# Another start, load order and instruction order for a squared-relu attention with a mixture of adapters

## The chip, the core and the metric

The kernel runs on one core of a Trainium2 chip. The core has five engines with instruction streams of their own: TensorE (PE, matmuls; its weight loads are listed as PEld), VectorE (DVE), ScalarE (ACT), GpSimd (POOL) and SyncE (SP). POOL, ACT and SP also issue DMA transfers. The metric is the device time of one execution in microseconds; lower is better. The kernel before takes 186.77 us, the median of 13 runs from 185.96 to 189.39.

## The reference

```python
# q, k, v: (8, 12, 448, 64) float32
scores = (1 / sqrt(64)) * q @ k.T                 # per batch and head: 448 x 448
attn   = maximum(scores, 0) ** 2 / 448
x      = (attn @ v), heads side by side            # (3584, 768)

logits = x @ w_gate                                # (3584, 8)
top two experts of each row, w = softmax over the two
out    = x + sum over the two: w[e] * (x @ A[e]) @ B[e]     # A: (8, 768, 16), B: (8, 16, 768)
```

## The kernel before, in words

**Tiling.** A head has 448 rows, split as 7 pieces (J) of 64. Twelve heads are taken four at a time, so there are 8 batches x 3 quads, each a "quad" (b, q) of four heads. A quad's q, k and v each come by one pair of DMA transfers from POOL, cast from fp32 to bf16 on the way (L271). A quad has seven steps, one for each 64 keys; the 168 steps are called chunks below.

**One quad.** PE transposes q and k, 56 matmuls of 64x64 against an identity (L386), and DVE copies the result from PSUM to the tile qT (L400). For each chunk PE computes the scores of four heads, four matmuls of 64x448 (L445), into a pair of PSUM banks. A relu with a scale brings them to SBUF as bf16, tile a (on ACT L465, on DVE L467). DVE squares two or three chunks at a time (L483). PE multiplies the squares with v, four matmuls a chunk (L500), adding up over the seven chunks, and two copies bring the sum to xt (L529, DVE or ACT).

**The adapters.** Two blocks of 36 small matmuls (L338) put A and w_gate, which come as a_raw and g_raw (L323, L325), in their places, by a selection matrix sel that POOL makes (L316, L317); a copy (L345) follows each block. For every 128 rows of x there is a gate product (six matmuls, L546), a few small DVE and ACT steps for the top two (L567 to L590), a transpose (L607) with a copy (zT, L616), and two output halves: three identity matmuls that bring x back (L634), one fp32 matmul with B (L639, which the profile shows as two), a copy to the tile osb (L656), and after both halves two stores from SP's queue (L666). There are 28 such row tiles, so 56 output halves.

**The first quad.** The first three pieces of k (CUT = 3) come uncast by one transfer each on SP's and ACT's queues into raw (L283), and DVE casts them to k_first (L298). The other four come by POOL with the cast into k_rest (L294). ACT loads its table with a sigmoid on a small tile (L287); POOL makes the identity.

**What sets the order.** The program is written as a list of operations with engines, assumed durations, dependencies, buffers taken and given back, and a rank (the chunk for which it is due, with offsets from the table C). A planner, `schedule`, plays this list forward on assumed costs and emits each engine's instructions in the resulting order; each engine then runs in that order. So a different rank, cost or pool size changes the order everywhere. Tile pools bound how far ahead anything runs: q and k 4 buffers, v 6, output tiles 6. The eight PSUM banks are handed out by the planner (scores take pairs). At most four load pairs are in flight (`lane=4`).

Loads are issued on POOL in the order of this loop; a tile of v follows the q and k of the next quad:

```python
    for i in range(len(tiles_of) + 1):
        if i < len(tiles_of):
            loads(i, 0)
            loads(i, 1)
        if i:
            loads(i - 1, 2)
        if i == 2:
            # sel, a_raw and g_raw, B
```

Of the kernel before, what the change touches and what calls it, by code (L numbers as in the profile page):

```python
# [13 lines left out]

J = 7
CUT = 3
PH = 64
QUADS = 3
NB = 8
S = J * PH  # L20
# [10 lines left out]
def parts(*cuts):  # L31
# [3 lines left out]

C = dict(
    tp_=2.3287, qk_=-3.679, sq_=3.7975, pv_=3.3372, xt_=-1.2131, gate_=-0.65203, id_=-0.78412,
    out_=-0.80943, zt_=6.6019, a12=(4, 7), late=6, merge_x=0, id2=2.6063, ocap=3, sqs=(2, 2, 3),
    slack=0.12309, switch=3.3127, third=4.3408, dve_relu=0.55845, relu_until=400, qk=-2.3217, sq=10,
    pv=1.0506, xt=8.4423, tp=-9.2867, tpe=4.3867, gate_mm=-4.8593, gate=-1.4524, zt=0.2432, zte=2.902,  # L40
    id=15.183, out=3.032, pace=6.5353,
)
POOLS = dict(qT=5, a1=C["a12"][0], a2=C["a12"][1], zp=2, zT=3, osb=6, w=3, q=4, k=4, v=6)

MODE_SWITCH = 0.13
HOP = 0.05
RAW = {"PE": 0.0, "ACT": 0.2, "DVE": 0.115, "POOL": 0.0, "SP": 0.0}
LAT = {"PE": 0.18, "ACT": 0.19, "DVE": 0.084, "POOL": 0.0, "SP": 0.0}
# [28 lines left out]
class Dma:  # L77


    def __init__(self, rate=0.4):  # L80
        self.rate, self.free = rate, 0.0

    def land(self, t, mb):
        self.free = max(self.free, t + 0.5) + mb / self.rate
        return self.free + 1.4


def schedule(ops, c=C):

    free = {e: 0.0 for o in ops for e in o.engs}
    avail = {e: [] for e in free}
    level = dict(POOLS, lane=4)
    freed = {b: 0.0 for b in range(c.get("nb", 8))}
    used = {"s": 0, "t": 0, "p": 0, "m": 0, "y": 0, "o": 0}
    cap = {"s": 3, "t": 1, "p": 2, "m": 2, "y": 1, "o": c.get("ocap", 1)}
    events, returns = [0.0], []
    dma = Dma()
    mode = None  # L100
    relus = []
# [13 lines left out]
    def choose(o):  # L115
        k, n = o.want
        if used[k] >= cap[k]:
            return None
        slots = sorted((x for x in range(0, c.get("nb", 8), 2) if x in freed and x + 1 in freed),
                       key=lambda x: max(freed[x], freed[x + 1]))  # L120
        if k == "s":
            if used["s"] >= 2 and any(
                x.want and x.kind != "qk" and x.ready <= t + 1e-9 and x.rank <= o.rank + c["third"]
                for x in avail["PE"]
            ):
                return None
            return [slots[0], slots[0] + 1] if slots else None
        halves = sorted((x for x in freed if x ^ 1 not in freed), key=lambda x: freed[x])
        if n == 1 and halves:
            return halves[:1]  # L130
        busy = c.get("nb", 8) // 2 - len(slots) - used["s"]
        if not slots or busy >= c.get("nb", 8) // 2 - 2:
            return None
        if n == 1 and busy == 1 and any(
            x.want and x.ready <= t + 1e-9 and x.kind in ("pv", "tp") and x.rank <= o.rank
            for x in avail["PE"]
        ):
            return None
        return [slots[0], slots[0] + 1][:n]
# [19 lines left out]
    while left:  # L159
# [9 lines left out]
        for e in free:  # L169
# [8 lines left out]
                    st = max(t, free[e] + MODE_SWITCH)  # L178
                mode = o.mode
            o.start, o.eng = st, e  # L180
            free[e] = st + o.dur[e]
            if o.kind == "load":
                o.end = dma.land(free[e], o.mb) + (o.lat or 0.0)
            else:
                o.end = free[e] + (LAT[e] if o.lat is None else o.lat)
            for x in o.engs:
# [41 lines left out]
def build(k=None, c=C):  # L228
# [49 lines left out]
    def first():  # L278

        def dma(eng, g):
            eng.dma_start(out=k.raw[g * PH : g * PH + PH], in_=k.qkv[1][0, g, :, 0:2, : CUT * PH])  # L283

        def warm():
            nc.vector.memset(k.warm, 0.0)
            nc.scalar.activation(k.warm, k.warm, ACTF.Sigmoid)  # L287

        def ident():
            make_identity(nc, k.identf)  # L290

        def rest():
            for g in range(2):
                nc.gpsimd.dma_start(out=k.k_rest[g * PH : g * PH + PH],  # L294
                                    in_=k.qkv[1][0, g, :, 0:2, CUT * PH :])

        def cast():
            nc.vector.tensor_copy(k.k_first, k.raw)  # L298

        ds = [op(("SP",), 0.8, lambda: dma(nc.sync, 0), kind="load", rank=-50.0),  # L300
              op(("ACT",), 0.8, lambda: dma(nc.scalar, 1), kind="load", rank=-50.0)]
        for d in ds:
            d.mb = 2 * CUT * PH * 64 * 4e-6
        op(ACT, 1.4, warm, rank=-49.0)
        q0 = load(0, 0, 0, [])
        oi = op(("POOL",), 0.6, ident)
        ob = op(DVE, 0.2, lambda: nc.vector.tensor_copy(k.identb, k.identf), deps=[oi], rank=-60.0)
        k0 = op(DVE, dve(2 * CUT * PH, 1.92), cast, deps=ds + [ob], rank=-50.0)
        k1 = op(("POOL",), 1.17, rest, kind="load", take=("lane",), give=("lane",))
        k1.mb = 4 * (S - CUT * PH) * 64 * 4e-6  # L310
        return q0, k0, k1


# [62 lines left out]
    def tp(b, q):  # L376
# [34 lines left out]
        if (b, q) == (0, 0):  # L411
            kw = dict(mode="64", kind="tp")
            m1 = op(PE, 0.1, lambda: mm(m1, 1, 0, CUT), deps=[loaded[b, 1, q][0]], ni=8 * CUT, banks=("s", 2),
                    take=("qT",), rank=-52.0, **kw)
            m = op(PE, 0.225, lambda: mm(m, 0), deps=[loaded[b, 0, q]], after=m1, ni=56, banks=("t", 2),
                   rank=-51.0, **kw)
            m2 = op(PE, 0.13, lambda: mm(m2, 1, CUT), deps=[loaded[b, 1, q][1]], after=m, ni=8 * (J - CUT),
                    banks=("s", 2), give=("q",), rank=-8.0, **kw)
            e1 = op(DVE, dve(2 * CUT * PH, 1.92), lambda: piece(nc.vector.tensor_copy, m1, 1, 0, CUT), deps=[m1],
                    free=[(m1, None)], rank=-42.0)  # L420
            es = [op(x, {"ACT": act(S), "DVE": dve(S, 1.92)},
                     lambda cp=cp, g=g: piece(cp, m, 0, 0, J, g), deps=[m, e1], free=[(m, g)], rank=-41.0)
                  for g, (x, cp) in enumerate(((DVE, nc and nc.vector.tensor_copy), (ACT, nc and nc.scalar.copy)))]
            e2 = op(DVE, dve(2 * (J - CUT) * PH, 1.92), lambda: piece(nc.vector.tensor_copy, m2, 1, CUT, J),
                    deps=[m2, es[0]], free=[(m2, None)], rank=-5.0)
            return [[e1, *es] + [e2] * (j >= CUT) for j in range(J)]
        m = op(PE, 0.225, lambda: mm(m, 0), deps=[loaded[b, 0, q]], mode="64", kind="tp", ni=56,
               banks=("t", 2), take=("qT",), rank=rank)
        m1 = op(PE, 0.225, lambda: mm(m, 1), deps=[loaded[b, 1, q], m], after=m, mode="64", kind="tp", ni=56,
                give=("k", "q"), rank=rank - 0.5)  # L430
        e = op(DVE, dve(4 * S, 1.92), ev, deps=[m1], free=[(m, None)], rank=rank + c["tpe"])
        return [[e]] * J

# [189 lines left out]
    def outputs(tl):  # L623
# [3 lines left out]
        v = due[tl]  # L627
        W = 64 * DO
        evs, obs, prev = [], {}, None
        for h in range(2):  # L630

            def f_b(h=h):
                for x in range(3):
                    nc.tensor.matmul(  # L634
                        out=bank(obs[h])[:, x * 128 : x * 128 + 128],
                        lhsT=k.xt[:, 3 * h + x, c0 : c0 + 128], rhs=k.identb,
                        start=(x == 0), stop=False, skip_group_check=True,
                    )
                nc.tensor.matmul(  # L639
                    out=bank(obs[h])[:, :W], lhsT=T["zT", g0][:, zi], rhs=k.B[:, h * W : h * W + W],  # L640
                    start=False, stop=True, skip_group_check=True,
                )

            last = False
            if h:
                zuse[g0] -= 1
                last = zuse[g0] == 0
            prev = op(PE, 0.81, f_b, mode="128", kind="b", deps=[o_zT, b_load] + xdeps[tl], after=prev,
                      banks=("o", 1), take=() if h else ("osb",), give=("zT",) if last else (),
                      rank=v + at("id", v) + (c["id2"] if h else 0), ni=10)  # L650
            obs[h] = prev

            def ev(cp, h=h):
                if ("osb", tl) not in T:
                    new("osb", ("osb", tl), [128, 128 * DO], F32)
                cp(T["osb", tl][:, h * W : h * W + W], bank(obs[h])[:, :W])  # L656

            evs.append(evac(W, ev, deps=[prev], free=[(prev, 0)], rank=v + at("out", v)))

        def st():  # L660
            r = 0
# [18 lines left out]
        if (b, w, q) not in loaded:  # L680
            loaded[b, w, q] = load(b, w, q, [])

    for i in range(len(tiles_of) + 1):
        if i < len(tiles_of):
            loads(i, 0)
            loads(i, 1)
        if i:
            loads(i - 1, 2)
        if i == 2:
            sel_op = op(("POOL",), 1.5, sel_fn)  # L690
            a_load = op(("POOL",), 1.5, aw_fn, kind="load")
            a_load.mb = 0.4
# [4 lines left out]

    groups, t = [], 0
    while t < NT:
        m = min(3, NT - t)  # L700
        if NT - t == 4:
            m = 2
        if t == NT - 2:
# [41 lines left out]
            finish(n - c["late"] - 1)  # L745
    for n in range(NS - c["late"] - 1, NS):
        finish(n)
    return ops


@with_exitstack
def kernel(
# [31 lines left out]
    h.a_raw = const.tile([128, E, DO, R], BF16)  # L784
    h.g_raw = const.tile([128, DO, E], BF16)
    h.raw = const.tile([128, 2, CUT * PH], F32)
    h.k_first = const.tile([128, 2, CUT * PH], BF16)
    h.k_rest = const.tile([128, 2, (J - CUT) * PH], BF16)
    h.warm = const.tile([1, 8], F32)
# [39 lines left out]
```

## Time and profile before

| | |
|---|---|
| median of 13 runs | 186.77 us |
| the profiled execution's own time | 186.99 us |
| its span, first to last instruction | 185.2 us |
| PE busy | 169.0 us (91%) |
| DVE busy | 159.2 us (86%) |
| ACT busy | 161.0 us (87%) |
| first scores on PE, first relu on ACT | 6.10 us, 6.91 us |
| last scores on PE | 160.16 us |
| last relu on ACT | 160.81 us |
| last output copy | 180.24 us |

The profile cuts the span into 40 slices of 4.63 us and gives the busy share of each engine in tenths. PE, DVE and ACT are all close to full between about 40 and 160 us; before that none of them is, and behind it PE alone is. A group row gives line, engine, operation, tiles, shape and count, then busy time and the mean duration of one, then the engine's idle time just before it and what ended that. A timeline row gives start and duration in us first. A busy PE is not a PE at its peak, since the ends of matmuls are modelled.

### The profile page before, as it was taken

The numbers are of one execution on the slowest core, as the hardware profiler recorded it, in microseconds if no ns is written. First come the engines' busy times: TensorE is split into PE (matmuls) and PEld (weight loads), VectorE is DVE, ScalarE is ACT, GpSimd is POOL, SyncE is SP. The second block draws the span as 40 slices with busy tenths as digits, with TensorE's granted clock in tenths as the row PEclk, the third lists the DMA queues.
The fourth block names the chain that finished last, engine by engine and source line by source line (L and its number), as shares of the span: only waits on it lengthen the run. The fifth ranks groups of instructions, "written<-read, shape, count | busy, mean of one in ns | idle before, by whom it ended". The sixth has DMA issues, their size and how long they took to land.

```text
span 185.2 us, 7480 instructions
## 1 busy us (share of the span) xinstructions
PE 169.0 (91%) x3236; PEld 99.4 (54%) x3236; DVE 159.2 (86%) x249; ACT 161.0 (87%) x234; POOL 90.8 (49%) x155
## 2 busy tenths in 40 slices
PE   0869998789999999999999999999999999999990
PEld 0526765445555646564656465655665566556640
DVE  1569999899999999999999999999999999853600
ACT  3677799899999999999999999999999999954350
POOL 7999789898786856465735744671100000000000
PEclk9999999999999999999999999999999999999996
DMA  5999999999999999799999999899430333344775
GB/s 92 122 168 145 177 161 176 178 182 177 143 232 228 223 185 243 118 175 170 174 186 133 192 185 200 118 193 228 89 86 2 88 88 90 85 106 110 210 196 147
DMA packets 26801, 28.71 MB, mean 155 GB/s; under 512 B 4432, under 2 KB 23120, under 8 KB 26768
## 3 DMA queue, kind: packets, MB, share of 16 engines
q0 software_dynamic: 22000, 17.03, 65.3%
q1 hardware_dynamic: 4624, 11.11, 20.3%
q8 instruction: 25, 0.41, 0.9%
q10 hardware_dynamic: 144, 0.10, 0.2%
q14 instruction: 8, 0.07, 0.1%
HBM read 33.84 MB, written 11.01 MB: 242 GB/s over the span
## 4 chain that ended last, share of the span: by engine, by line
PE 57%; DVE 16%; ACT 13%; issue 4%; POOL 4%; DMA 3%; ACTq 0%; POOLq 0%
PE ps L639 17%; PE ps L445 13%; ACT a L465 12%; PE ps L500 12%; DVE a L483 8%; PE ps L634 6%; PE ps L546 4%; DMA q<-in_q_dram 3%; PE ps L386 3%; DVE qT L400 3%; DVE xt L529 3%; PE ps L338 2%; POOL q L271 1%; PE ps L607 1%; DVE zp L590 1%
## 5 line engine op out<-in xcount | busy, mean ns | idle before, releaser
L465 ACT ACTIVATE a<-ps 128x896 bf16<-128x896 f32 x162 | 139.1, 955 | 5.2 <-PE ps L445 4.9
L483 DVE TENSOR_TENSOR a<-a 128x1792 bf16<-128x1792 bf16 (+1 forms) x72 | 88.3, 1247 | 0.4 <-ACT a L465 0.4
L445 PE MATMUL ps<-qT 64*64 64x448 bf16 x672 | 61.5, 378 | 4.0 <-ACT a L465 2.0
L639 PE MATMUL ps<-B,zT 128*128 128x384 f32 x112 | 48.4, 514 | 0.0
L500 PE MATMUL ps<-a,v 64*64 64x448 bf16 x672 | 44.0, 358 | 0.6 <-DVE qT L400 0.5
L271 POOL DMA_DIRECT2D v<-in_v_dram x48 | 29.1, 621 | 27.2 <-PE ps L500 12.7
L445 PEld LDWEIGHTS <-qT 64*64 64x64 bf16 x672 | 23.5, 107 | 34.4 <-issue 25.6
L271 POOL DMA_DIRECT2D q<-in_q_dram x48 | 29.2, 626 | 8.9 <-PE ps L386 2.4
L271 POOL DMA_DIRECT2D k<-in_k_dram x46 | 28.2, 637 | 3.0 <-PE ps L445 1.9
L500 PEld LDWEIGHTS <-v 64*64 64x64 bf16 x672 | 22.3, 109 | 12.1 <-issue 5.1
L656 ACT COPY osb<-ps 128x384 f32<-128x384 f32 x45 | 22.3, 495 | 7.0 <-PE ps L639 5.9
L529 DVE CAST xt<-ps 128x448 bf16<-128x448 f32 x42 | 24.9, 618 | 3.6 <-PE ps L500 3.2
L400 DVE COPY qT<-ps 128x1792 bf16<-128x1792 bf16 x23 | 24.9, 1083 | 2.1 <-PE ps L386 1.4
L634 PE MATMUL ps<-identb,xt 128*128 128x128 bf16 x168 | 18.8, 221 | 0.1
L634 PEld LDWEIGHTS <-xt 128*128 128x128 bf16 x168 | 11.3, 97 | 13.2 <-issue 11.5
L639 PEld LDWEIGHTS ps<-B,zT 128*128 128x128 f32 x112 | 16.9, 191 | 0.0
L546 PE MATMUL ps<-awg,xt 128*128 128x136 bf16 x168 | 13.4, 224 | 0.0
L386 PEld LDWEIGHTS <-q 64*64 64x64 bf16 x672 | 10.6, 114 | 4.3 <-DMA q<-in_q_dram 1.5
L546 PEld LDWEIGHTS <-xt 128*128 128x128 bf16 x168 | 10.1, 98 | 4.8 <-issue 4.4
L386 PE MATMUL ps<-identb,k 64*64 64x64 bf16 x644 | 11.0, 199 | 1.5 <-DMA k<-in_k_dram 1.5
L386 PE MATMUL ps<-identb,q 64*64 64x64 bf16 x672 | 11.0, 199 | 0.4
L386 PEld LDWEIGHTS <-k 64*64 64x64 bf16 x644 | 9.4, 110 | 3.0 <-DMA k<-in_k_dram 2.5
(41 smaller groups left out, 72.2 us busy)
## 6 DMA issues: line engine op xcount, KB each, us to landing
out_dram<-osb SPq DMA_DIRECT2D x56, 192.0 KB, 3.4
q<-in_q_dram POOLq DMA_DIRECT2D x48, 112.0 KB, 4.7
v<-in_v_dram POOLq DMA_DIRECT2D x48, 112.0 KB, 4.6
k<-in_k_dram POOLq DMA_DIRECT2D x46, 112.0 KB, 5.0
B<-in_moe_B_dram POOLq DMA_DIRECT2D x1, 384.0 KB, 5.6
a_raw<-in_moe_A_dram POOLq DMA_DIRECT2D x1, 192.0 KB, 5.6
k_rest<-in_k_dram POOLq DMA_DIRECT2D x2, 64.0 KB, 2.9
raw<-in_k_dram ACTq DMA_DIRECT2D x1, 96.0 KB, 2.6
```

Source lines behind the costliest of these rows:

```text
L271: nc.gpsimd.dma_start(out=t[g * PH : g * PH + PH], in_=k.qkv[w][b, g, :, 2 * q : 2 * q + 2, :])
L386: nc.tensor.transpose(k.ps_b[sl * PH : sl * PH + PH, o.banks[g], (w * J + j) * PH : (w * J + j) * PH + PH], source(w, j)[r, sl], k.identb[ ...
L400: nc.vector.tensor_copy(t.rearrange("p g w x -> p g (w x)"), k.ps_b[:, m.banks[0] : m.banks[0] + 2, : 2 * S])
L445: nc.tensor.matmul(out=bank(o, sl)[g * PH : g * PH + PH, at : at + w], lhsT=t[r, g, 1, j * PH : j * PH + PH], rhs=t[r, g, 0, x0:x1], start ...
L465: nc.scalar.activation(out, flat(qk_ops[n], w), ACTF.Relu, scale=k.relu_scale)
L483: nc.vector.tensor_mul(a2, T["a1", g0], T["a1", g0])
L500: nc.tensor.matmul(out=bank(head, g)[sl * PH : sl * PH + PH, :w], lhsT=vn[r, sl, j * PH : j * PH + PH], rhs=T["a2", g0][r, i, sl * w : sl ...
L529: evac(w, lambda cp, g=g: cp(k.xt[:, g * QUADS + q, b * S + x0 : b * S + x1], bank(src, g)[:, :w]), deps=[pv_ops[n]], free=[(src, g)], ran ...
L546: nc.tensor.matmul(out=bank(zops[0])[:, t * ZW : t * ZW + ZW], lhsT=k.xt[:, do, 128 * tiles[t] : 128 * tiles[t] + 128], rhs=k.awg[:, do, : ...
L634: nc.tensor.matmul(out=bank(obs[h])[:, x * 128 : x * 128 + 128], lhsT=k.xt[:, 3 * h + x, c0 : c0 + 128], rhs=k.identb, start=(x == 0), sto ...
L639: nc.tensor.matmul(out=bank(obs[h])[:, :W], lhsT=T["zT", g0][:, zi], rhs=k.B[:, h * W : h * W + W], start=False, stop=True, skip_group_che ...
L656: cp(T["osb", tl][:, h * W : h * W + W], bank(obs[h])[:, :W])
```

## The change

At the start, PE multiplies a tile of zeros eight times (`SPIN`) before the first transposes, and eight shorter times between the transposes of the first q and the first scores. The last four pieces of the first k come uncast by two transfers on ACT's queue, behind ACT's table load, and DVE casts them. POOL's loads run in the order q_0, q_1, k_1, q_2, k_2, v_0, and so on: v comes one quad later, sel and a_raw two turns of the loop later. A quad's q transposes now wait for its k as well (`tboth`). Output tiles have 4 buffers instead of 6; q and k 5 instead of 4, v 7 instead of 6. The planner gets other costs for the start and for loads, four other weights, offsets to the ranks of 84 operations, and fixed engines for 12.

```diff
+SPIN = 8
-    out_=-0.80943, zt_=6.6019, a12=(4, 7), late=6, merge_x=0, id2=2.6063, ocap=3, sqs=(2, 2, 3),
-    slack=0.12309, switch=3.3127, third=4.3408, dve_relu=0.55845, relu_until=400, qk=-2.3217, sq=10,
+    out_=-0.80943, zt_=6.6019, a12=(4, 7), late=6, merge_x=0, id2=2.6063, ocap=3, tboth=1, sqs=(2, 2, 3),
+    slack=0.097658, switch=4.846, third=4.5956, dve_relu=0.45964, relu_until=400, qk=-2.3217, sq=10,
-POOLS = dict(qT=5, a1=C["a12"][0], a2=C["a12"][1], zp=2, zT=3, osb=6, w=3, q=4, k=4, v=6)
+POOLS = dict(qT=5, a1=C["a12"][0], a2=C["a12"][1], zp=2, zT=3, osb=4, w=3, q=5, k=5, v=7)
+RANKS = {
+    1: -6, 148: -7, 163: -106, 166: -110, 171: 27, 175: -64, 180: -17, 187: -31, 197: -44, ...
+}
+ENGINES = {
+    170: "DVE", 214: "DVE", 315: "DVE", 330: "DVE", 337: "ACT", 446: "DVE", 547: "DVE", ...
+}
+BEGIN = {"PE": 1.1, "ACT": 0.74, "DVE": 0.8, "POOL": 1.24, "SP": 0.74}
+COLD = 7.0
...
-            free[e] = st + o.dur[e]
+            free[e] = st + o.dur[e] * (2 if e == "PE" and st < COLD else 1)
...
+        def zeros():
+            nc.vector.memset(k.zeros, 0.0)
+        def spin():
+            for _ in range(SPIN):
+                nc.tensor.matmul(k.ps[:, 7, :], lhsT=k.zeros[:, :128], rhs=k.zeros, start=True, stop=True)
         def rest():
             for g in range(2):
-                nc.gpsimd.dma_start(out=k.k_rest[g * PH : g * PH + PH],
-                                    in_=k.qkv[1][0, g, :, 0:2, CUT * PH :])
+                dma(nc.scalar, k.raw_rest, g, CUT, J)
...
+        k1 = op(DVE, dve(2 * (J - CUT) * PH, 1.92), lambda: nc.vector.tensor_copy(k.k_rest, k.raw_rest),
+                deps=[kr], rank=-30.0)
...
+            def spin():
+                for _ in range(2):
+                    for g in range(2):
+                        for sl in range(2):
+                            nc.tensor.matmul(bank(sp, g)[sl * PH : sl * PH + PH, :], lhsT=k.zeros[g * PH : g * PH + PH, :PH],
+                                             rhs=k.zeros[g * PH : g * PH + PH], start=True, stop=True)
...
-    for i in range(len(tiles_of) + 1):
+    for i in range(len(tiles_of) + 2):
         if i < len(tiles_of):
             loads(i, 0)
             loads(i, 1)
-        if i:
-            loads(i - 1, 2)
-        if i == 2:
+        if i > 1:
+            loads(i - 2, 2)
+        if i == 4:
             sel_op = op(("POOL",), 1.5, sel_fn)
...
+    for i, d in RANKS.items():
+        ops[i].rank += d / 4
+    for i, e in ENGINES.items():
+        ops[i].engs = (e,)
```

In the order that comes out, PE begins with eight zero matmuls, the transposes of k_first and q_0, eight short zero matmuls, the scores of chunks 0 to 2, then the transposes of q_1, k_rest and k_1, the scores of chunks 3 to 6, the transposes of q_2 and k_2, and the scores of six chunks of the second quad. Before, it took the second quad's transposes and the first quad's scores in turns: q_1 after chunk 3, k_1 after chunk 5.

## The prediction

> **What bounds the kernel now.** I read, in this order: the page's table of busy time and its 40 slices; the timeline of ACT up to 45 us and the waits there; the groups of PE instructions cut into short windows; busy time by stage; the chain of waits.
>
> ```profile
> PE 169.0 (91%) x3236; PEld 99.4 (54%) x3236; DVE 159.2 (86%) x249; ACT 161.0 (87%) x234; POOL 90.8 (49%) x155
> ...
> PE   0869998789999999999999999999999999999990
> ...
> ACT  3677799899999999999999999999999999954350
> ...
> PEclk9999999999999999999999999999999999999996
> DMA  5999999999999999799999999899430333344775
> ```
>
> Three stages: to about 42 us no engine is full; from there to 160 PE, DVE and ACT are all full; after 160 only PE is. The first stage on ACT (start, duration, operation, and in brackets the idle time before it with its releaser):
>
> ```profile
> 6.91 4.16 ACT L465 ACTIVATE a<-ps 128x896 bf16<-128x896 f32 x5 [0.68 <-PE ps L445]
> 11.83 0.92 ACT L465 ACTIVATE a<-ps 128x896 bf16<-128x896 f32 x1 [0.77 <-PE ps L445]
> 13.24 4.33 ACT L465 ACTIVATE a<-ps 128x896 bf16<-128x896 f32 x5 [0.49 <-PE ps L445]
> ```
> ```profile
> 18.50 2.54 ACT L465 ACTIVATE a<-ps 128x896 bf16<-128x896 f32 x3 [0.93 <-PE ps L445]
> 22.01 1.73 ACT L465 ACTIVATE a<-ps 128x896 bf16<-128x896 f32 x2 [0.97 <-PE ps L445]
> 24.06 4.16 ACT L465 ACTIVATE a<-ps 128x896 bf16<-128x896 f32 x5 [0.32 <-PE ps L445]
> ...
> 33.21 0.92 ACT L465 ACTIVATE a<-ps 128x896 bf16<-128x896 f32 x1 [0.43 <-PE ps L445]
> 34.30 4.97 ACT L465 ACTIVATE a<-ps 128x896 bf16<-128x896 f32 x6 [0.17 <-PE ps L445]
> ```
>
> Each relu without a bracket follows the last at 0.81 to 0.83 us (five in 4.16 with a last one of 0.95). Each bracket is ACT waiting for PE's scores (L445). Between 13.24 and 42 these waits sum to 0.93 + 0.97 + 0.32 + 0.43 + 0.17 = 2.82 us. Why is PE late? Two reasons. It is slow (window 6 to 7 us, then 100 to 110 us, then the change-over):
>
> ```profile
> L445 PE MATMUL ps<-qT 64*64 64x448 bf16 x8 | 1.4, 557 | 0.4 <-DVE qT L408 0.4
> ```
> ```profile
> L445 PE MATMUL ps<-qT 64*64 64x448 bf16 x44 | 3.6, 355 | 0.0
> ```
> ```profile
> 16.70 1.38 PE L500 MATMUL ps<-a,v 64*64 64x448 bf16 x12
> ...
> 18.20 0.73 PE L500 MATMUL ps<-a,v 64*64 64x448 bf16 x8
> ```
>
> The same matmul takes 557 ns early and 355 later; from 18.2 us on it is fast. And PE waits for data:
>
> ```profile
> 10.84 0.58 PE L386 MATMUL ps<-identb,k 64*64 64x64 bf16 x26 [0.56 <-DMA k<-in_k_dram]
> ...
> 13.66 0.13 PEld L386 LDWEIGHTS <-q 64*64 64x64 bf16 x2 [0.86 <-DMA q<-in_q_dram]
> ```
>
> The DMA row is full from the second slice on, so early loads queue for bandwidth, not only for POOL's issue. The last stages (length; busy time and instruction count of PE, PEld, DVE, ACT, POOL; clock; DMA):
>
> ```profile
> 120.00:140.00 20.00, 19.99 (x413) 12.12 (x409) 19.79 (x33) 19.68 (x28) 4.76 (x8) 1.00 0.68 140
> 140.00:160.00 20.00, 20.00 (x361) 11.60 (x354) 19.61 (x31) 19.82 (x32) 0.00 (x0) 1.00 0.25 62
> 160.00:170.00 10.00, 10.00 (x99) 5.99 (x92) 5.80 (x16) 5.72 (x13) 0.00 (x0) 1.00 0.46 120
> ```
>
> So what is won early moves the whole front forward, and PE's own work from about 100 us on sets the end.
>
> **The change part by part.** A chunk below is one of the 168 steps of four L445 matmuls and a relu; seven make a quad.
>
> *Spin.* Eight 512-column matmuls on zeros, as soon as DVE has cleared the tile (DVE starts at 0.80, then idles until 3.18, so the memset is free). PE idles until 4.56 today; eight at the slow rate (448 columns take about 0.37 us per four there, so about 0.43 us for 512) are 3.4 us, 1.2 to 4.6: hidden by the wait for k_first, or 0.2 us late at worst. Eight short ones more stand between the q transposes and the first scores, where PE waits 0.45 us for the DVE copy: 0.4 us if PE is fast by then, 0.8 if slow, so up to 0.4 lost.
>
> *Does it release the clock?* Row first: PE was busy 4.16 of 5 us from 5 to 10, and matmuls stayed at 557 to 576 ns until 18.2, after the first dense stretch (12.6 to 18.1). The granted clock column says full throughout and does not show it. [...]
>
> *k_rest through ACT's queue, in fp32.* POOL loses two issues (1.21 us), so q_1, k_1 and everything behind are issued 1.2 us earlier. ACT gains two issues (its one takes 0.72), about 3.0 to 4.5 us, inside its idle time before 5.70. DVE gains one cast, 0.43 by the row of the 128x512 copy, inside its idle second before 7.12. The HBM bytes are the same, and the DMA row is full, so k_1, at 10.84 today, lands between 9.6 (issue decides) and 10.84 (bandwidth decides). I take the middle, 10.2.
>
> *Order of the start.* Now all of q_1, k_rest and k_1 are transposed ahead of chunks 3 to 6. First relu: 6.91 less about 0.3 for faster scores, 6.6. ACT does two and DVE one, and both are through by 8.7. k_1 at 10.2, its transposes 0.4, scores 0.4: chunk 3 at 11.0, four chunks (one on DVE) to 13.5. The next quad's scores stand behind the transposes of q_2 and k_2. Those of k_2 started at 14.68 today; without v ahead (about 1.5 us per load pair, two loads from 10.84 to 13.98) and 0.6 earlier they have data at about 13.0: scores at 13.5, relu at 13.9. Today that quad starts at 13.24: **0.65 lost**.
>
> *After that.* With PE at full speed four scores cost 0.19 instead of 0.37, 56 transposes about 0.5 instead of 1.2, and 12 scores stand ahead of each block of 36 weight matmuls (8 or fewer today, the 0.97 stall), so the 2.82 us of waits go: **2.82 won**. What is late next is a_raw: POOL now reaches it after k_0 and v_1, at about 15.8 instead of 14.20, and with the same 5.6 us it lands at 21.4 (19.8 today). PE is in order: chunk 18 stands behind those 36 matmuls (1.6 us) and is there at 23.6, while ACT is through chunk 17 at 22.95: **0.65 lost**. The later v costs nothing: no product with it stands before chunk 13.
>
> *Searched order.* Counting changes between 64-row and 128-row matmuls up to the last scores: 128 before, 113 after; behind chunk 105, where PE is the bound, 58 and 50. Price, from the chain of waits:
>
> ```profile
> 103.61 0.50 PE ps L445 x8
> ...
> 107.83 0.38 PE ps L445 x8
> ```
>
> Eight scores after a 128-row run take 0.12 more: 8 x 0.12 = **1.0 won**. Work left behind the last scores: 17 output halves instead of 18; they were only moved, so I count nothing more. DVE takes three more relus (3 x 1.08), seven more output copies and nine fewer xt copies; but eleven of its output copies now lie behind the last relu (three today). So up to there DVE has +3.2 - 0.6 - 5 = about 2 us less, and ACT, by the same count, about 1 more (three relus and a few zT copies less, some eight xt and three output copies more). Both are full there: I take zero, and keep +-1. The output buffers fall from 6 to 4: a tile lives 1.0 (two copies) + 1.1 (two issues) + 2.6 (landing) = 4.7 us, and a new one comes every 1.8 us at the end, so four last 7.2: free, unless stores take over 5 us. Deeper q, k, v buffers: POOL's waits of 27 us before v are cover, nothing.
>
> *Sum.* -2.82 - 1.0 + 0.65 + 0.65 = -2.5, and -0.1 for the earlier first relu: -2.6 on the profiled 186.99 us (span 185.2) gives 184.4; that execution is 0.2 above the median, so **184.2**.
>
> **The rivals.** About 0.3% (0.6 us) is what a measurement here tells from no change.
>
> *More than that* (0.25): k_1 at 9.6 and a_raw in time, so nothing is lost at the start (0.65 + 0.65), and all 15 changes of mode count (1.8): -4.8, **181.9**. For it: PE is 99% busy from 40 us. Against: the full DMA row.
>
> *The clock is not kept* (0.12): then most of the 2.82 stays, and -1.0 + 1.3 - 0.5 leaves -0.2: **186.5**. For it: the 2 us hole before k_1, and how long today's gappy start stayed slow.
>
> *ACT starves in the full stage* (0.13): from 45 to 160 us ACT waits 0.2 us for scores in all, so a new order can only lose there. Fewer changes of mode mean longer runs between scores (three output halves in a row, 2.6 us, against two or three chunks of cover, 1.6 to 2.4). It decides from 2.6 us over 18 quads, 0.15 per quad; at 0.2 per quad it costs 3.8: +1.2, **188.0**. Against: what was done by chunk 42, 84, 126 is nearly the same in both orders.
>
> **How the numbers follow.** Likeliest (0.50): 184.2, own range 182.4 to 186.0 (k_1 at 9.6 or 10.84, the +-1 of DVE). With the rivals 181.0 to 187.3 leaves out about 2 in 10. Faster 0.81: the first two and half of the third; same 0.06; slower 0.13.
>
> **What would show it.** Right: L445 at about 355 ns by 8 us; no ACT wait for scores over 0.5 us between 14 and 42 but one near 23; the second quad's first relu near 13.9; last scores near 158, not 160.2. Wrong: 557 ns after 10 us; ACT waits of 1 us and more between 45 and 160; PE waiting for a_raw beyond 22; evictions waiting for stores in the last 20 us.

## The result, and the profile after

The kernel after takes **184.82 us** (median of 11 runs, 183.85 to 185.92); the kernel before took 186.92 (48 runs over all comparisons). The ratio is 0.9885, with a 95% interval from 0.9861 to 0.9909: faster by 2.1 us. The profiled execution takes 184.17 us (span 182.4) against 186.99 (span 185.2), which is 2.82 us less. They lie 0.65 below and 0.07 above their medians, so the 2.82 (by chance also the sum of the prediction's waits) is used below to find places, and the 2.1 as the size.

The busy time and the rows of the page after:

```profile
PE 167.0 (92%) x3252; PEld 100.6 (55%) x3252; DVE 163.6 (90%) x255; ACT 156.4 (86%) x230; POOL 88.7 (49%) x153
...
PE   7678897789999999999999999999999999999990
...
ACT  3459999999999999999999999999999999941200
...
PEclk9978999999999999999999999999999999999999
DMA  5999999999999999998999999982340335153775
```

PE is busy from the first slice on (zeros), ACT's last work falls one slice earlier, and from the fourth slice ACT is full. New is the 7 and 8 in PEclk: from 11.8 to 15.2 us PE's clock was taken back. ACT's timeline after (start, duration, operation; in brackets the idle time before it with its releaser):

```profile
1.49 1.28 ACT L309 ACT_TABLE_LOAD   x1 [1.49 <-PEq L892]
1.55 1.26 ACTq L306 DMA_DIRECT2D raw_rest<-in_k_dram  x2
...
6.37 0.53 ACT L441 COPY qT<-ps 128x448 bf16<-128x448 bf16 x1 [3.37 <-PE ps L419]
7.37 1.73 ACT L519 ACTIVATE a<-ps 128x896 bf16<-128x896 f32 x2 [0.47 <-PE ps L499]
11.05 15.73 ACT L519 ACTIVATE a<-ps 128x896 bf16<-128x896 f32 x19 [1.95 <-PE ps L499]
26.96 4.96 ACT L519 ACTIVATE a<-ps 128x896 bf16<-128x896 f32 x6 [0.18 <-PE ps L499]
```

The first relu comes later than before (7.37, not 6.91) and ACT then waits 1.95 us. But once chunk 3 starts at 11.05, nineteen relus follow without a break, and up to 45 us ACT waits for scores 0.18 us more. Before, it waited 2.82 us between 14 and 42 us. The start is one longer hole, then nothing.

How far the front is can be read from the squares, which run in order (the microsecond, named by its end, in which the n-th of DVE's 72 square instructions starts):

| n | 4 | 8 | 16 | 28 | 40 | 56 | 68 | 72 |
|---|---|---|---|---|---|---|---|---|
| before | 17 | 26 | 43 | 69 | 93 | 127 | 155 | 163 |
| after | 16 | 24 | 41 | 66 | 91 | 125 | 152 | 161 |

About 2 us are won before 26 us and then kept: the 24 squares from the 16th to the 40th, and the 32 from there to the 72nd, take the same time in both to within a microsecond. The end, on PE (last scores; last matmul with B) and DVE (last output copy):

```profile
158.46 0.36 PE L499 MATMUL ps<-qT 64*64 64x448 bf16 x4
...
176.56 0.86 PE L694 MATMUL ps<-B,zT 128*128 128x384 f32 x2
```
```profile
177.47 0.56 DVE L726 COPY osb<-ps 128x384 f32<-128x384 f32 x1 [0.31 <-PE ps L694]
```

Last scores at 158.46 instead of 160.16 (-1.7). From there to PE's last end it is 18.96 us instead of 20.04 (-1.1): 17 output halves of 0.87 us are left, not 18.

### The profile page after: what moved, and what is told of

Same layout as the page of the kernel before. It is cut to its first block, busy times and chain, and to the rows that moved or that the text cites. A ratio compares the mean times of both kernels' runs of the same rounds, so it can differ in the third digit from the quotient of the medians.

```text
span 182.4 us, 7497 instructions
## 1 busy us (share of the span) xinstructions
PE 167.0 (92%) x3252; PEld 100.6 (55%) x3252; DVE 163.6 (90%) x255; ACT 156.4 (86%) x230; POOL 88.7 (49%) x153
## 4 chain that ended last, share of the span: by engine, by line
PE 39%; ACT 24%; DVE 24%; issue 8%; DMA 2%; POOL 0%; ACTq 0%; DVEq 0%; POOLq 0%
ACT a L519 21%; PE ps L694 15%; DVE a L537 12%; PE ps L499 8%; PE ps L554 6%; PE ps L689 5%; DVE qT L433 5%; DVE xt L583 3%; PE ps L419 2%; DMA q<-in_q_dram 2%; PE ps L600 2%; ACT osb L726 2%; DVE osb L726 1%; DVE zp L644 1%; PE ps L661 1%
## 5 line engine op out<-in xcount | busy, mean ns | idle before, releaser
L519 ACT ACTIVATE a<-ps 128x896 bf16<-128x896 f32 x159 | 137.5, 994 | 2.8 <-PE ps L499 2.8
L499 PE MATMUL ps<-qT 64*64 64x448 bf16 x672 | 58.0, 366 | 5.3 <-ACT a L519 3.2
L499 PEld LDWEIGHTS <-qT 64*64 64x64 bf16 x672 | 24.6, 105 | 35.6 <-issue 27.5
L554 PE MATMUL ps<-a,v 64*64 64x448 bf16 x672 | 43.0, 350 | 0.9 <-ACT a L519 0.4
L554 PEld LDWEIGHTS <-v 64*64 64x64 bf16 x672 | 21.9, 106 | 8.8 <-issue 1.8
L433 DVE COPY qT<-ps 128x1792 bf16<-128x1792 bf16 x23 | 24.9, 1083 | 0.3 <-ACT a L519 0.3
L726 ACT COPY osb<-ps 128x384 f32<-128x384 f32 x38 | 19.9, 554 | 3.1 <-PE ps L694 3.1
L583 DVE CAST xt<-ps 128x448 bf16<-128x448 f32 x33 | 19.6, 618 | 1.7 <-PE ps L554 1.5
L689 PEld LDWEIGHTS <-xt 128*128 128x128 bf16 x168 | 11.6, 97 | 13.8 <-issue 11.5
L726 DVE COPY osb<-ps 128x384 f32<-128x384 f32 x18 | 10.0, 556 | 3.6 <-PE ps L694 3.3
L600 PEld LDWEIGHTS <-xt 128*128 128x128 bf16 x168 | 10.3, 98 | 5.1 <-issue 4.4
L419 PEld LDWEIGHTS <-q 64*64 64x64 bf16 x672 | 10.1, 110 | 3.9 <-issue 1.3
L419 PE MATMUL ps<-identb,q 64*64 64x64 bf16 x672 | 10.3, 195 | 1.2 <-DMA q<-in_q_dram 0.7
```

The source lines that it names most:

```text
L419: nc.tensor.transpose(k.ps_b[sl * PH : sl * PH + PH, o.banks[g], (w * J + j) * PH : (w * J + j) * PH + PH], source(w, j)[r, sl], k.identb[ ...
L433: nc.vector.tensor_copy(t.rearrange("p g w x -> p g (w x)"), k.ps_b[:, m.banks[0] : m.banks[0] + 2, : 2 * S])
L499: nc.tensor.matmul(out=bank(o, sl)[g * PH : g * PH + PH, at : at + w], lhsT=t[r, g, 1, j * PH : j * PH + PH], rhs=t[r, g, 0, x0:x1], start ...
L519: nc.scalar.activation(out, flat(qk_ops[n], w), ACTF.Relu, scale=k.relu_scale)
L554: nc.tensor.matmul(out=bank(head, g)[sl * PH : sl * PH + PH, :w], lhsT=vn[r, sl, j * PH : j * PH + PH], rhs=T["a2", g0][r, i, sl * w : sl ...
L583: evac(w, lambda cp, g=g: cp(k.xt[:, g * QUADS + q, b * S + x0 : b * S + x1], bank(src, g)[:, :w]), deps=[pv_ops[n]], free=[(src, g)], ran ...
```

## The experiments

The theory at this point: the order in which q_0, the rest of k, k_1 and k_2 arrive sets the start; the zeros and the clock matter little. The rivals: the zeros and the fast clock carry the gain; or the searched order does. Line numbers of variants are shifted by a few lines: in variants of the kernel after, L499 to L505 are the scores, L519 to L526 the relu and L554 and L556 the products with v; in those of the kernel before, L447 and L467 are the scores and the relu.

**1. The zeros alone, in the kernel before.**

```diff
+    nc.vector.memset(h.zeros, 0.0)
+    for _ in range(8):
+        nc.tensor.matmul(h.ps[:, 7, :], lhsT=h.zeros[:, :128], rhs=h.zeros, start=True, stop=True)
     for o in schedule(build(h)):
         o.fn()
```


> The kernel before with the eight zero matmuls put ahead of everything, its own order untouched. Theory 1 (the gain is made at the start, by fast matmuls together with the earlier loads and the new order): matmuls fast by about 8 us, the waits of ACT between 13 and 42 us shrink from 2.8 to about 1.5 us, time 0.7 to 1.2 us under before. Theory 2 (the searched order alone carries the gain, data arrive too late for a fast PE to matter): within 0.4 us of before. Theory 3 (the clock alone carries it): about 2 us under before.

Measured: 187.6 us, ratio 1.0055 (1.003 to 1.0081): slower, which none of the three theories had. Windows of PE (length, busy and count, granted clock, DMA share, GB/s), and its wait for nothing that shows:

```profile
8.00:10.00 2.00, 1.36 (x38) 0.74 1.02 132
10.00:12.00 2.00, 1.12 (x34) 0.50 1.21 173
...
16.00:18.00 2.00, 2.00 (x28) 0.50 1.47 239
18.00:20.00 2.00, 2.00 (x31) 0.70 1.16 189
```
```profile
PE ps L386 <- issue: 0.9, 1, 0.9
```

The clock was released early (26 transposes in 0.41 us from 8.65; first relu 6.82), but taken back at about 9, with PE 69 and 56% busy in the two microseconds before, and not given again before 19.2. Eight waits of ACT between 12 and 33 us remained (0.20 to 0.93 each), and PE stood 0.9 us on "issue". In the old order the zeros are no gain.

**2. The kernel after without the zeros.**

```diff
     for o in schedule(build(h)):
-        o.fn()
+        if o.kind != "spin":
+            o.fn()
```


> The kernel after with both blocks of zero matmuls left out, every other instruction in the same order. Theory 1: matmuls at 557 ns to 18 us or later, ACT waits again for scores between 14 and 30 us, time 1.0 to 1.8 us over the kernel after (about 185.8 to 186.6). Theory 2: within 0.4 us of the kernel after. Theory 3: about 2 us over it, no faster than before.

Measured: 185.21 us, ratio 0.9929 (0.9893 to 0.9965), profiled span 183.0. ACT's timeline, then PE's scores from 6 to 10, and its scores and products from 14 to 18 us (count; busy, mean ns; idle before):

```profile
8.06 1.73 ACT L519 ACTIVATE a<-ps 128x896 bf16<-128x896 f32 x2 [0.68 <-PE ps L499]
...
12.00 20.46 ACT L519 ACTIVATE a<-ps 128x896 bf16<-128x896 f32 x25 [2.21 <-PE ps L499]
```
```profile
L499 PE MATMUL ps<-qT 64*64 64x448 bf16 x12 | 1.5, 568 | 0.4 <-DVE qT L441 0.4
```
```profile
L499 PE MATMUL ps<-qT 64*64 64x448 bf16 x24 | 2.6, 532 | 0.2 <-ACT a L519 0.2
L554 PE MATMUL ps<-a,v 64*64 64x448 bf16 x24 | 1.3, 352 | 0.4 <-ACT a L519 0.4
```

PE's scores are slow here (568 ns from 6 to 10, 575 from 10 to 14, 532 on the mean from 14 to 18 us, against 355 from 6 to 10 in the kernel after), and yet 25 relus run without a break. So fast scores up to there are not what removed the waits after chunk 3. The first products, ahead of 18 us, are fast again (352 ns), so the run does not show what slow products would cost (runs 5 and 6 do). What the zeros are worth is small: 0.4 us by the medians, 0.8 by the ratios (whose intervals overlap, so it is not clear of noise), 0.6 by the spans, and in the trace it is chunk 3 (12.00 against 11.05).

**3. Filling the hole, so that the clock is kept.** 28 short matmuls on zeros stand ahead of the transposes of k_1, where PE idles.

```diff
+        def hold():
+            for _ in range(7):
+                for g in range(2):
+                    for sl in range(2):
+                        nc.tensor.matmul(k.ps[sl * PH : sl * PH + PH, m.banks[g], 224:], ...)  # zeros
-        m1 = op(PE, 0.225, lambda: mm(m, 1), deps=[loaded[b, 1, q], m]
+        m1 = op(PE, 0.225, lambda: (hold() if (b, q) == (0, 1) else None, mm(m, 1)), ...
```


> The kernel after with 28 more zero matmuls (about 0.85 us) in the hole where PE waits for k_1, before k_1's transposes. If the half-speed stretch from 11.9 to 15.1 us comes from that hole, the clock column stays at 1.00 there, and scores take about 355 ns throughout. As ACT has no wait there, the time stays within 0.4 us; if the half-speed stretch costs, it falls by 0.4 to 0.8 us.

Measured: 186.02 us, ratio 0.994 (0.991 to 0.9971): slower than the kernel after, which was not expected. PE's windows after, without the filling:

```profile
8.00:9.00 1.00, 0.40 (x23) 1.00 1.23 174
9.00:10.00 1.00, 0.41 (x26) 1.00 1.11 152
10.00:11.00 1.00, 0.39 (x8) 1.00 1.21 178
11.00:12.00 1.00, 0.77 (x12) 0.92 1.24 191
12.00:13.00 1.00, 1.00 (x61) 0.50 1.22 191
```

And with it, three of these windows, then PE's timeline:

```profile
9.00:10.00 1.00, 1.00 (x56) 1.00 1.24 179
10.00:11.00 1.00, 0.23 (x11) 1.00 1.22 194
...
12.00:13.00 1.00, 0.70 (x43) 1.00 1.18 182
```
```profile
13.54 0.32 PE L419 MATMUL ps<-identb,k 64*64 64x64 bf16 x17 [0.81 <-issue]
...
30.09 0.24 PE L419 MATMUL ps<-identb,k 64*64 64x64 bf16 x5 [1.16 <-issue]
```

With the zeros in it (all of the stretch from 9 to 10 busy) the clock stays at 1.00 to 31.5 us; without, it falls just before 12. These are two single executions, and run 12, with the hole unfilled, kept its clock to 22.1 us (28 products in 1.52 from 15.27 on), so the hole can cost the clock and need not; on what it hangs stays open. Keeping it buys nothing: chunk 3 comes at 11.26, and the added instructions came with two idle times on "issue" of 2.0 us together, each followed by a wait of ACT (0.32 and 0.88); what makes them stays open. Even the five fastest of the 12 executions, with mean granted clocks of 0.998 to 1.00, took 185.28 to 185.56 us.

**4. The rest of k really behind the table load.** A short sigmoid that writes into the tile holds each transfer back.

```diff
             for g in range(2):
+                nc.scalar.activation(k.raw_rest[g * PH : g * PH + 1, 0, :8], k.warm, ACTF.Sigmoid)
                 dma(nc.scalar, k.raw_rest, g, CUT, J)
```


> The kernel after with its two raw_rest transfers made to wait for an ACT instruction behind the table load, so that they are issued at about 3.1 and 4 us instead of 1.55. If raw_rest held back q_0's second half (5.88 us, 5.07 before), that half lands near 5.1 and the first relu starts near 6.6 instead of 7.37; k_rest comes later, about 7.5 to 8. Chunk 3 still waits for k_1 and its copies, so the time changes by under 0.4 us. If the first relu set the time, it would be 0.7 us under the kernel after.

Measured: 186.19 us, ratio 0.9983 (0.9956 to 1.001): 1.4 us slower than after by the medians, where less than 0.4 was expected. (Its profiled execution, 188.22 us, lies above its median, so only its first 15 us are read.) Its DVE and ACT timelines:

```profile
10.70 0.49 DVE L343 CAST k_rest<-raw_rest 128x512 bf16<-128x512 f32 x1 [4.55 <-DMA raw_rest<-in_k_dram]
```
```profile
14.22 0.92 ACT L520 ACTIVATE a<-ps 128x896 bf16<-128x896 f32 x1 [5.47 <-PE ps L500]
```

Issued at 3.26 and 4.15, the slower of the two transfers took 6.4 us to land, and the cast stood until 10.70; in the kernel after, the two issued at 1.55 and 2.19 took 4.0 to 4.7, and the cast began at 6.96. POOL's loads of k_1, issued at 4.28 and 4.86, were late here too: 5.8 to 6.0 us, against 4.2 to 4.5 in the kernel after. In return q_0 came sooner (first relu 7.02). The early issue during the table load is worth more than it takes from q_0.

**5. The rest of k back on POOL, with the cast, in the kernel after.**

```diff
-                dma(nc.scalar, k.raw_rest, g, CUT, J)
+                nc.gpsimd.dma_start(out=k.k_rest[g * PH : g * PH + PH], in_=k.qkv[1][0, g, :, 0:2, CUT * PH :])
...
+    move("k_rest", behind="q 0 0"); move("ident", behind="q 0 0")      # the cast on DVE goes
```


> The kernel after with k_rest loaded as before, by POOL with the cast, between the identity and q_1; no transfers on ACT's queue behind raw and no cast on DVE. If raw_rest held back q_0's second half, that half lands near 5.1 us and the first relu starts near 6.7; k_1, issued 1.2 us later, lands at 9.7 to 10.8 instead of 9.41. By the theory that the start is set by k_1 and the copies behind it, chunk 3 starts at 11.1 to 12 and the time is 0 to 0.8 us over the kernel after. If the early q_0 counts more, it is up to 0.5 us under it.

**6. v_0 back ahead of q_2 and k_2, in the kernel after.**

```diff
+    move("v 0 0", behind="k 0 1")      # on the planned list; all else keeps its order
```


> The kernel after with one edit to POOL's order: v_0's two loads back ahead of q_2 and k_2, as before. PE's order is unchanged, so the second quad's scores still stand behind the transposes of q_2 and k_2. If the later v is what lets that order go without waits, q_2 and k_2 land about 1.5 us later, the ACT run that begins at 11.05 breaks near 13.6 us with a wait of 1 to 1.5 us, and the time rises by 0.8 to 1.4 us (185.6 to 186.2). If loads are not what the front waits for after 11 us, it stays within 0.3 us.

Measured: 186.46 us, ratio 0.9983 (0.9952 to 1.0014), and 186.21 us, ratio 0.998 (0.9958 to 1.0002). Undoing either one alone gives back most of the gain: 1.6 (0.8 at most was expected) and 1.4 us by the medians, 1.8 by the ratios; 1.0 and 0.8 against run 9, the kernel after but for one pool size, which ran beside them. ACT and PE of the fifth, then PE and ACT of the sixth:

```profile
6.89 1.73 ACT L524 ACTIVATE a<-ps 128x896 bf16<-128x896 f32 x2 [0.47 <-PE ps L504]
...
14.66 4.96 ACT L524 ACTIVATE a<-ps 128x896 bf16<-128x896 f32 x6 [1.56 <-PE ps L504]
```
```profile
13.67 0.58 PE L424 MATMUL ps<-identb,k 64*64 64x64 bf16 x26 [1.31 <-DMA k<-in_k_dram]
```
```profile
14.13 0.58 PE L421 MATMUL ps<-identb,k 64*64 64x64 bf16 x26 [1.28 <-DMA k<-in_k_dram]
```
```profile
15.13 4.96 ACT L521 ACTIVATE a<-ps 128x896 bf16<-128x896 f32 x6 [1.35 <-PE ps L501]
```

The same picture in both: k_2 comes 1.3 to 1.8 us later than in the kernel after (there its transposes start at 12.37 without a wait), PE, which runs in order, waits for it, and ACT misses the second quad by 1.4 to 1.6 us. The fifth even starts sooner (first relu 6.89, as before), since its q_0 comes sooner (its transposes run through from 4.90, where the kernel after waits 0.73 for it); and still it loses. The second quad's first relu comes at 14.66 and 15.13, against 13.63 in the kernel after: about 1.0 and 1.5 us are lost by k_2 directly.

A second part of the loss goes with the clock. It was taken back at 12.5 and 12.2 us, and given again only at 19.3 and 22.4 (11.8 and 15.2 in the kernel after); in the 3.41 us behind the loss PE, waiting for k_2, was busy only 58 and 62%, against 92%. The first 28 products then ran slow, and ACT waited for the scores behind them a second time. The kernel after, then PE and ACT of the sixth:

```profile
16.22 1.52 PE L554 MATMUL ps<-a,v 64*64 64x448 bf16 x28 [0.43 <-ACT a L519]
```
```profile
17.72 2.83 PE L556 MATMUL ps<-a,v 64*64 64x448 bf16 x28 [0.22 <-ACT a L521]
```
```profile
20.97 4.16 ACT L521 ACTIVATE a<-ps 128x896 bf16<-128x896 f32 x5 [0.87 <-PE ps L501]
```

In the fifth the 28 products took 2.53 us, and ACT waited 0.39 (at 20.02). Its executions differ in this too: the four fastest of 12, 185.34 to 185.61 us, had mean granted clocks of 0.976 to 0.979; five of the six slowest, 186.95 us and more, had 0.968 to 0.972. So most of the gain lies in k_2 by 12.4 us, in part directly and in part through a clock that comes back sooner; no run separates the two.

**7. v later alone, in the kernel before** (v_0 behind k_2 on POOL, all else in its order).

```diff
+    move("v 0 0", behind="k 0 2")
```


> The kernel before with one edit to POOL's order: the first v tile's two loads moved behind those of q_2 and k_2; every engine's other instructions as before. If the plain load order carries the early gain by itself, q_2 lands about 1.5 us earlier (PE waited for it 0.86 us at 13.66) and 0.5 to 1 us come off the time. If the gain needs PE's new order as well, the time stays within 0.4 us of before, or v_0 is late for the first products at 16.0 and it is up to 0.7 us slower.

Measured: 186.74 us, ratio 0.9972 (0.9942 to 1.0001): no gain clear of noise. ACT's timeline:

```profile
13.05 6.59 ACT L467 ACTIVATE a<-ps 128x896 bf16<-128x896 f32 x8 [0.50 <-PE ps L447]
21.64 1.73 ACT L467 ACTIVATE a<-ps 128x896 bf16<-128x896 f32 x2 [2.00 <-PE ps L447]
```

Eight relus run through where a wait of 0.93 us stood (at 18.50), then it comes back at 21.64 (2.00 instead of 0.97). PE reaches the first block of weight matmuls sooner but stands 1.10 us before it: it starts at 19.56, against 19.93 before, and a_raw landed only at 19.42. The old order has the scores of 16 chunks ahead of that block, the new one 18. (The clock came at 15.7 us here instead of 18.5, and the first 20 products took 1.14 us instead of 2.08; that, too, can have removed the 0.93.) A later v pays only with an order that has other work in that place.

**8. The kernel after without the searched offsets and engine choices.**

```diff
-    (the two loops that apply RANKS and ENGINES to the operations)
```


> The kernel after without the 84 rank offsets and the 12 fixed engines; the planner orders the rest by its table. Theory 1: the start is as good, the tail or the middle gives back 0.5 to 1 us (185.3 to 185.8). Theory 2: all of the gain goes, 186.5 to 187.

Measured: 192.07 us, ratio 1.0299 (1.0263 to 1.0335), far outside both expectations. Its start is nearly the same (chunk 3 at 11.65, and no wait of ACT from there to 24.9), though in its profiled run ACT stood 0.69 us before the first relu, as with the slow scores of a_nospin (0.68), and not 0.47; it falls behind from 24 us on, and from 45 to 160 us PE waits 3.0 us for relus. So the new pools and costs need the offsets to be as good as before. This does not say what the search won over the order before, which had offsets of its own.

**9. Six output tiles instead of four** (order unchanged).

```diff
-bufs=POOLS[p]))
+bufs=6 if p == "osb" else POOLS[p]))
```


> The kernel after with six output tiles instead of four, the order unchanged. A tile lives about 4.7 us and a new one comes every 1.8 us at the end, so four should never make a copy wait: the time stays within 0.3 us. If stores hold the tiles longer, it falls by 0.3 to 0.8 us.

Measured: 185.44 us, ratio 0.9947 (0.9909 to 0.9984); no gain over the kernel after (0.9885). The start has no output tiles yet, and still its first relu came at 7.74 instead of 7.37 (q_0 later), so part of the difference is one of arrivals; differences of about half a per cent between runs at different times are not read here. Four tiles cost nothing that shows.

**10 to 12. A better start?** The transposed rest of k stands ready, but DVE copies it only after its first square. Ten moves that copy ahead; eleven also moves k_1's transposes behind chunk 4's scores; twelve is ten with the two blocks of weight matmuls moved back. In twelve the moved blocks write a PSUM bank of scores ahead of its relu, so part of the result changes, and it is read for its waits only.

```diff
+    move("sq 0", behind="k_rest copy")                                   # all three
+    move("tk 0 1", behind="qk 4"); move("tc 0 1", behind="tk 0 1")       # eleven
+    move("aw 0", behind="qk 20"); move("aw 1", behind="qk 25"); ...      # twelve
```


> The kernel after with two DVE instructions swapped: the copy of k_rest's transposes (10.14 us) ahead of the first square (9.13). If ACT's 1.95 us wait before chunk 3 is set by that copy, chunk 3 starts at about 10.3 instead of 11.05 and the time falls by 0.6 to 0.8 us. If arrivals (k_1, then k_2) set the front a little later anyway, the wait only moves and the time stays within 0.3 us.

> As a_copyfirst, and the transposes and the copy of k_1 stand behind the scores of chunk 4 instead of ahead of chunk 3, so that chunk 3 no longer waits for k_1. If standing behind k_1 is what costs at the start, chunk 3 starts at about 9.2 to 9.5 us and the time falls by 1.3 to 1.8 us under the kernel after (to about 183.2). If k_1's copy then comes late for the second quad, a wait of about 1 us appears near 12 us and 0.3 to 0.8 us remain.

> The kernel after with the copy of k_rest's transposes ahead of the first square, and the two blocks of 36 weight matmuls (with their copies) moved behind the scores of chunks 20 and 25, where they stood behind those of 17 and 20. With the copy alone the front won 0.9 us at chunk 3 and lost it by 22.7 us, where PE waited 0.46 us for a_raw and ACT 0.54 us for scores. If a_raw is what took it back, that wait goes and the time falls 0.5 to 0.9 us under the kernel after. If the front is held at the same place by another arrival (q_0, k_0 of the next batch) or by DVE, it stays within 0.3 us.

Measured: 184.6 us, ratio 0.9871 (0.9834 to 0.9908); 184.91 us, ratio 0.9894 (0.985 to 0.9938); 187.34 us, ratio 1.0025 (0.9993 to 1.0057). Ten cannot be told from the kernel after. Its ACT and PE:

```profile
10.18 2.74 ACT L524 ACTIVATE a<-ps 128x896 bf16<-128x896 f32 x3 [1.00 <-PE ps L503]
...
22.68 9.02 ACT L524 ACTIVATE a<-ps 128x896 bf16<-128x896 f32 x11 [0.54 <-PE ps L503]
```
```profile
20.60 0.22 PE L372 MATMUL ps<-a_raw,sel 128*128 128x128 bf16 x1 [0.46 <-DMA a_raw<-in_moe_A_dram]
```

Chunk 3 is won 0.87 us earlier (0.51 of it is left at the eighth relu), and given back when PE reaches the weights before a_raw is there. In twelve, the same ACT timeline shows that a_raw was the stop, and that it cannot just be passed:

```profile
10.25 13.88 ACT L526 ACTIVATE a<-ps 128x896 bf16<-128x896 f32 x17 [1.04 <-PE ps L505]
25.19 2.77 ACT L526 ACTIVATE a<-ps 128x896 bf16<-128x896 f32 x3 [1.06 <-PE ps L505]
```

Seventeen relus run past 22.7, then the 36 matmuls stand in the way at 25.19. In eleven's profiled run PE was still slow behind the zeros (26 transposes in 0.58 us from 6.15; first relu 8.01) and to 17.1 us, so whether its move is of use stays open; its median shows no gain. No variant was clearly faster than the kernel after.

## Why the prediction was right, and which steps were not

184.2 was predicted and 184.82 measured; on the profiled execution 184.4 and 184.17. The three large terms of the sum, however, sit partly in other places. (The sum of the first rival comes out at 182.0, not 181.9; nothing hangs on it.)

- **Spin, hidden.** Right: 1.19 to 4.79, and the first transposes of k at 4.72 (4.56 before).
- **The clock is kept.** Half wrong. That the zeros bring full speed by 8 us, and that it lasts through the wait for k_1, was my estimate; no run from before the forecast shows it. In its place the kernel after showed full speed by about 6 us (26 transposes in 0.41 from 5.88) and half speed from 11.8 to 15.2. PE did not stand idle ahead of the loss: it was 39 to 77% busy in each of the four microseconds before, and 49% over the last 3.41 us (last section). The rival that the clock is not kept was priced at +2.4, and that price was too high for this order: ACT does not feel the loss (no wait of note between 11.05 and 26.8), and a_nospin, with scores slow past 14 us (532 ns on the mean to 18), loses 0.4 to 0.8. Where the clock stays away longer it does cost (runs 5 and 6).
- **First relu 6.6.** Wrong: 7.37. ACT's two issues were counted as issue time only. The transfers started at 1.55, during the table load and not behind it, and shared the transfers with q_0, whose second half came at 5.88 instead of 5.07. Putting k_rest back on POOL brings 6.89.
- **Chunk 3 at 11.0.** 11.05, for another reason: k_1 came at 9.41 (10.2 was predicted), but DVE's copy of k_rest's transposes stood behind the first square, which I had not counted:

```profile
9.13 1.09 DVE L537 TENSOR_TENSOR a<-a 128x1792 bf16<-128x1792 bf16 x1 [0.21 <-ACT a L519]
10.14 0.42 DVE L441 COPY qT<-ps 128x512 bf16<-128x512 bf16 x1
```
```profile
10.61 0.76 PE L499 MATMUL ps<-qT 64*64 64x448 bf16 x12 [0.80 <-DVE qT L441]
```

- **Second quad, 0.65 lost.** The mechanism held (k_2 as the last arrival), the size was less: k_2's transposes started at 12.37 and not 13.0, and that quad's first relu at 13.63, a loss of 0.4. (The 14.68 of the prediction for the kernel before is the first weight load; the transposes themselves started at 15.05.)
- **2.82 won because PE is fast.** The waits went, all but 0.18. The reason given is wrong in the main: with the zeros out and the scores slow past 14 us (run 2) they go as well. It is the early k_2 (runs 5, 6) and the scores planned ahead of the weights (run 7); a fast clock behind 16 us has a part in it (runs 5, 6) that is not measured alone. The count of scores was misread, too: just ahead of the first block stand 12 before as well (8 and 4), and what differs is the chunks scored by then, 16 and 18.
- **a_raw, 0.65 lost.** Not there: POOL issued it at 14.20 as before. One load pair more stands ahead of it (1.2 us), but the making of sel took 0.83 us instead of 1.75, and a wait of 0.23 for a load to land fell away; PE began with it at 20.59 and ACT did not wait. Run 10 shows the cover is thin.
- **Changes of mode, 1.0 won.** Not there: the squares from the 48th to the 72nd take 52 us in both. What I counted at nothing, one output half fewer behind the last scores, shows as -1.1 in the tail. The same size in another place; the sum was right in part by luck.
- **Costs at nothing.** Four output tiles (run 9) and the balance of DVE and ACT (0.2 us of waits for scores from 45 to 158 us in both) held, so the rival of a starved ACT fell.

Still open: what the searched order is worth against the order before, and the deeper pools of q, k and v alone; how the loss in runs 5 and 6 divides between k_2 and the clock; and the idle time on "issue".

## What to carry to other kernels

At a start where one engine runs in order and loads arrive in a row, list for each load when its first user reaches the head of the queue, and judge every edit by the last arrival (here k_2), not by the first (the first relu got 0.46 us later and the kernel still won). Moves of loads pay together with an order that has other work in the place of the moved one: the late v alone gave 0.3% at most, all of the change 1.2%. Warming a clock by empty work is worth what the slow clock costs on the path, so measure that first; here it was 0.4 to 0.8 us of 187. And look at the clock of every variant: a late load also leaves PE idle, and in runs 5 and 6 the clock then stayed away longer (6.8 and 10.2 us, against 3.4) and cost a second time.

## What the runs showed of the hardware

- In the kernel after the trace's record of the granted clock begins at 5.00 us, falls to half at 11.83 and is full again at 15.24: 6.83 and 3.41 us lie between. The half speed lasted about 3.4 us in a_hold (from 31.5), a_osb6 and a_copyfirst too, about 6.8 in a_krest_pool and a_rest_late, and about 10.2 in b_spin (8.9 to 19.2) and a_vearly. PE's busy time in pieces of 3.41 us, as the profile models it, in the kernel after and then in run 11 (length; busy and count; clock; DMA):

```profile
1.59:5.00 3.41, 3.41 (x22) 1.00 0.86 170
...
8.42:11.83 3.41, 1.68 (x60) 1.00 1.18 173
11.83:15.24 3.41, 3.15 (x80) 0.50 1.13 165
```
```profile
0.05:3.46 3.41, 2.27 (x6) 1.00 0.25 52
3.46:6.87 3.41, 2.46 (x48) 1.00 1.21 224
```

- In the kernel after PE was busy in all of the 3.41 us ahead of 5.00, and 26 transposes took 0.41 us from 5.88 on. In run 11 it was busy 66 and 72% in the two pieces above, the 26 transposes took 0.58 us from 6.15, and PE was slow to 17.1 us. In the kernel before it was busy 84, 74 and 72% in the three pieces from 4.87 to 15.11, and eight scores took 0.98 us from 14.32 on; it was busy in all of the piece from 15.11 to 18.52, and eight scores took 0.57 from 18.74 on. What decides these runs do not settle.
- PE did not stand idle ahead of the loss of the clock in the kernel after (49% busy in the 3.41 us before 11.83). Run 12, with the same hole, kept its clock: 28 products took 1.52 us from 15.27, as with the full clock of the kernel after at 16.22, and the weight matmuls took 0.27 instead of 0.22 only from 22.1 us on. What decides stays open.
- In the kernel before scores took 557 ns from 6 to 7 us and 355 from 100 to 110, while the clock column showed 1.00 for both. The 0.50 of the column in the kernel after, from 11.83 to 15.24, came behind a fast stretch.
- A transfer that stands behind the table load in ACT's program was issued at 1.55, inside the load (1.49 to 2.77). An instruction writing to the same tile held it back to 3.26 (a_rest_late).
- A transfer on ACT's queue that was issued after POOL's loads were under way took up to 6.4 us to land in a_rest_late's profiled execution, against 4.0 to 4.7 in the kernel after, where it was issued ahead of most of them.
- More instructions on PE at the start came with idle times on "issue": 0.9 us in b_spin, 0.81 and 1.16 in a_hold.
